# Exponentials by heads and the bound on v on ScalarE, pooled q and k by products, and a new table of priorities

## The chip, the cores and the metric

The program runs on one core of one Trainium2 chip. The metric is the device time of one execution in microseconds; the kernel before took 1002.84 us (median of three runs, 1001.24 to 1004.5). The engines are PE (TensorE matrix products, with PEld for its weight loads), DVE (VectorE), ACT (ScalarE), POOL (GpSimd) and SP (SyncE, which issues the DMAs). SBUF is the working memory; PSUM has eight banks, into which PE writes.

## The reference, cut to what matters

The input is four batches of 8 heads, 576 positions, head width 64. Attention has two branches that are added; two expert layers follow.

```
q_d, k_d, v_d = means of q, k, v over groups of 4 positions      # 144 pooled positions
out_d     = softmax(q_d k_d^T / 8) v_d,  each row repeated 4 times
out_local = softmax(q k^T / 8, only where |i - j| < 4) v
x = out_up + out_local                     # 2304 tokens x 512
x = ((x w_a) * (x w_b)) w_out              # d_ff 1536
h = x w_in ; g = max(h,0) + alpha*min(h,0) ; out = g w_out2      # d_ff 2048
```

The weights are held in 64-bit words and are brought to 32-bit and then split in pairs of f16 parts inside the kernel.

## The kernel before, in words

**Attention.** A batch is cut in six tiles of 96 query positions (TQ), each with a window of 104 key positions (WK); 24 tiles in all, the first six being batch 0. For a tile, `turn` (line 678) transposes q and k on PE, ScalarE copies them out of PSUM, and VectorE sums each group of four positions into the pooled q and k. `bound` (line 693) takes the largest magnitude of v on VectorE. `soft` (line 707) adds the band mask and the eight heads' products in two PSUM banks, takes the row maxima on VectorE, subtracts them into SBUF, lets ScalarE do one exponential over 96x832, sums it on VectorE, and scales by the reciprocal. `p_turn` and `av_t` (lines 731 and 740) transpose the probabilities and multiply by v. When all six tiles of a batch are turned, `g_top`, `g_minus`, `g_exp` and `g_out` do the pooled branch, `od_turn` transposes its result, `batch_scale` (line 786) turns the bound on v into a power of two, and `x_add` (line 756) adds both branches and splits the sum with that scale into two f16 parts in `xt`.

**Expert layers.** `s1(j, f)` (line 925) takes 288 tokens j and 128 columns f of the first layer: 24 products into two banks, then two operations of ScalarE and two of VectorE. Blocks 0 and 1 are batch 0: block 0 is its tiles 0 to 2, block 1 its tiles 3 to 5. `wab_chunk(c)` (line 993) prepares the weights for columns 2c and 2c+1: per chunk, two times three integer passes over 128x1024 on VectorE, two squares with a sum on ScalarE, and a split of each half on ScalarE and VectorE. `wo_words` and `split_rows` prepare the second weights in a like manner; `s2`, `s3`, `s4` are the other three layers.

**Order.** All instructions are first recorded. `on(t, ...)` puts steps in a calendar by a nominal time; that sets the order in which they are recorded, so the turns in which steps take PSUM banks, SBUF rings and the single bank `r` that `top_of` (line 465) uses. `Plan` (line 26) then gives each step a duration by a formula, a priority from what depends on it plus the offset of its name in the table `URGENT` (line 291), and lists each engine's instructions in order. The products of the expert layers hang in one fixed chain: the order of the calendar (s1(0,0), s1(0,1), s1(1,0), s1(1,1), s1(0,2), ...). On the chip each engine runs its list in order and waits on semaphores. `Plan.fill` (line 257) puts unneeded bf16 products on the identity (tile names `m<-idf`) into gaps of PE that the plan foresees, in its first 200 us.

**Banks.** PSUM has four banks `m` (expert layers; `h`, for the first turns, is the first two of them; the fourth holds the pooled v), three banks `a` (attention) and one bank `r`. The first batch's steps have calendar places 0.6 apart in the sequence that begins at line 1123; in it `batch_scale(0)` has place 23.4. `wab_chunk` stands at 8 + 10c (line 1175), so chunk 0 at 8, chunk 1 at 18, chunk 2 at 28.

Of the kernel before, what the change touches and what calls it, by code (L numbers as in the profile page):

```python
# [25 lines left out]
class Plan:  # L26
# [101 lines left out]
    def __call__(self, eng, method, *args, **kw):  # L128
        if "out" in kw:
            writes, ins = [kw["out"]], [a for a in args if hasattr(a, "ap")]  # L130
        else:
            writes, ins = [args[0]], [a for a in args[1:] if hasattr(a, "ap")]
        out = writes[0]
        for k, a in kw.items():
            if k == "accum_out":
                if a is not None:
                    writes.append(a)
            elif k != "out" and hasattr(a, "ap"):
                ins.append(a)
        o = self.group  # L140
        if o is None or eng != self.PE:
            o = self.new(eng)
        if eng == self.SP:
            el = kw["in_"]
            parts = [int(c) for _, c in el.ap]
            nb = SIZE[el.dtype]
            for c in parts:
                nb *= c
            run = min(min(int(x.ap[-1][1]) for x in (kw["out"], kw["in_"])) * SIZE[el.dtype], 4096)
            rate = 230e3 if run >= 1024 else 150e3  # L150
            o.dma = (nb / rate, 2.2)
            o.dur += 1.0
        else:
            d, o.lag = self.cost(eng, method, out, ins, kw)
            o.dur += d
        for a in ins:
            if not self.external(a):
                o.reads.append(self.region(a))
        for a in writes:
            if not self.external(a):  # L160
                o.writes.append(self.region(a))
        f = getattr(getattr(self.nc, eng), method)
        o.calls.append((f, args, kw))
        if o is not self.group:
            self.close(o)
# [116 lines left out]
    def issue(self):  # L282
        for o in self.order:
# [4 lines left out]
WAY = (0,0,0,0,0)  # L288


URGENT = {"": -180, "alphas": -80, "bs0": -40, "bs1": 120, "bs2": 35, "bs3": 140, "gexp0": -20, "gexp1": -130,
# [31 lines left out]
def kernel(  # L323
# [40 lines left out]
    FAC = 4  # L364
# [29 lines left out]
    banks["h"] = banks["m"][:2]  # L394
    nbank = dict.fromkeys(banks, 0)

    def bank(tag):
        nbank[tag] += 1
        return banks[tag][(nbank[tag] - 1) % len(banks[tag])]
# [210 lines left out]
    odt = carve(KD * NP).rearrange("p (a n) -> p a n", a=KD)  # L610
    vd.append(carve(H * (D + 1))[:HALF].rearrange("p (h d) -> p h d", h=H))
# [16 lines left out]
    def setup1():  # L628
        for t, n in ((idf, 128), (idb, WK)):
# [11 lines left out]
          channel_multiplier=-1)  # L641

# [35 lines left out]
    def turn(i, tag):  # L678

        b, s0, kb, off = win(i)  # L680
        rq, rk, _ = raw_of(i)
        qz, kz = qk_of(i)
        t = i % TPB
        for src, n, dst, acc, o in ((rq, TQ, qz, gq_z[b % 2], 0), (rk, WK, kz, gk_z[b % 2], off)):
            ps = bank(tag)[:, :H2 * n].rearrange("p (a n) -> p a n", a=H2)
            with pe():
                for p in range(H2):
                    T("transpose", ps[:, p], src[:, p * 128:(p + 1) * 128], idf[:n, :n])
            A("copy", dst, ps)
            V("tensor_reduce", out=acc[:, :, t * TP:(t + 1) * TP],  # L690
              in_=dst[:, :, o:o + TQ].rearrange("p a (n r) -> p a n r", r=FAC), axis=AX.X, op=ALU.add)

    def bound(i):
        V("tensor_reduce", out=vst[win(i)[0] % 2][:WK, i % TPB:i % TPB + 1], in_=raw_of(i)[2], axis=AX.XY,
          op=ALU.max, apply_absolute_value=True)
# [11 lines left out]
    def soft(i, tag="a"):  # L707
# [5 lines left out]
        with pe():  # L713
# [3 lines left out]
            for h in range(H):  # L717
                T("matmul", pss[h % 2][:, h // 2], qz[rows(h), h // 2], kz[rows(h), h // 2], start=False,
                  stop=(h >= H - 2))
        for g in range(2):  # L720
            hs = slice(H2 * g, H2 * g + H2)
            V("tensor_reduce", out=m[:, hs], in_=pss[g], axis=AX.X, op=ALU.max)
            V("tensor_tensor", out=p[:, hs], in0=pss[g], in1=m[:, hs].unsqueeze(2).to_broadcast([TQ, H2, WK]),
              op=ALU.subtract)
        A("activation", out=p, in_=p, func=ACTF.Exp, scale=scale)
        V("tensor_reduce", out=z, in_=p, axis=AX.X, op=ALU.add)
# [13 lines left out]
    def av_t(i, tag="a"):  # L740

        ps = bank(tag)[:, :KD * TQ].rearrange("p (a n) -> p a n", a=KD)
        with pe():
# [4 lines left out]
    def od_turn(b, tag="a"):  # L748
        for u in range(2):
# [6 lines left out]
    def x_add(i):  # L756

        b, t = divmod(i, TPB)
        p0 = i * TQ % XR
# [26 lines left out]
    def batch_scale(b):  # L786
# [6 lines left out]
        pow2_abs(vm, sxb[b], us, up=-1)  # L793
# [328 lines left out]

    add(setup1)
    add(lambda: load(0))
    add(setup2)
    add(lambda: load(1))
    add(setup3)
    for i in range(2, TPB):
        add(lambda i=i: load(i))
    for i in range(3):  # L1130
        add(lambda i=i: wab_load(i))
# [16 lines left out]

    tops(0)
    turns(2)  # L1150
    rest(0)
    turns(3)
    tops(1)
    turns(4)
    rest(1)
# [5 lines left out]
    tops(2)  # L1161
    for n in range(3):
        add(lambda n=n: g_exp(0, n), "gexp0")
    rest(2)
# [3 lines left out]
    for i in range(3):  # L1168
        add(lambda i=i: x_add(i), f"x{i}")
    head_end = len(seq) * 0.6  # L1170
    for n, (fn, name, bias) in enumerate(seq):
        on(n * 0.6, fn, name, bias)
# [128 lines left out]
    def group(name):  # L1301
        kind = name.rstrip("0123456789")
        n = name[len(kind):]
        if kind in ("turn", "bound", "soft", "pturn", "av", "v", "x", "load") and n:
            b = int(n) // TPB
            return f"{kind}@{b}" if kind in ("x", "load") else f"t@{b}" if b else f"t0@{n}"
# [45 lines left out]
```

## Time and profile before

| | |
|---|---|
| median of three runs | 1002.84 us (1001.24 to 1004.5) |
| the profiled execution | 1003.87 us, its span 1002.1 us |
| PE busy | 977.7 us (98%), 7488 instructions |
| DVE busy | 608.3 us (61%), 1293 instructions |
| ACT busy | 434.4 us (43%), 919 instructions |
| POOL busy | 39.5 us (4%) |
| chain that ended last | PE 84%, DVE 13%, issue 1%, ACT 1% |

The span is the time from the first to the last instruction that the profiler recorded; the execution's time has 1.8 us more around it. Busy time is the union of an engine's instructions. PE's busy time holds the unneeded products of `fill`. All steps are issued from one helper, so every instruction has line 285, and instructions are told apart by the tiles that they write and read (`zone` is a large SBUF tile that holds many things; `nm` and `nz` are the softmax's maxima and sums; `vst` the bound; `sx` a batch's scale).

### The profile page before, as it was taken

Reading aid. Unit: us, or ns where it says so; the run is one execution under the profiler, and the core shown is the slowest. Engines: PE = TensorE matmul, PEld = TensorE weight load, DVE = VectorE, ACT = ScalarE, POOL = GpSimd, SP = SyncE. Lnnn points to the kernel's source line nnn. Section 1 sums busy time; section 2 is a strip of 40 time slices with the busy share of each in tenths; the row PEclk is TensorE's granted clock in tenths of the full one; section 3 lists DMA queues with packets and bytes.
Section 4 is the critical chain, followed back from the end, with each engine's and each line's share of the span. In section 5 each row is a group of like instructions: output and inputs, shape, how many; then the busy total and the mean of one; then the engine's idle time right before and its main releaser. Section 6 shows DMA issues by size and latency. Waiting matters only on the chain.

```text
span 1002.1 us, 18185 instructions
## 1 busy us (share of the span) xinstructions
PE 977.7 (98%) x7488; PEld 672.5 (67%) x7488; DVE 608.3 (61%) x1293; ACT 434.4 (43%) x919; POOL 39.5 (4%) x81
## 2 busy tenths in 40 slices
PE   6988999999999999999999999999999999999998
PEld 4666777778877788777877777645546455464553
DVE  6899999876657566678987585612406135061340
ACT  3335566544424343335435364623516235162350
POOL 3001300012000200000000000000000000000000
PEclk9999999999999999999999999999999999999999
DMA  9596451144201512323343401010100100200000
GB/s 204 159 270 173 108 153 42 26 75 86 50 1 25 111 26 58 102 67 109 111 159 129 130 1 48 1 43 22 32 32 1 43 22 9 78 2 11 22 1 31
DMA packets 95938, 69.45 MB, mean 69 GB/s; under 512 B 71152, under 2 KB 78704, under 8 KB 95856
## 3 DMA queue, kind: packets, MB, share of 16 engines
q1 hardware_dynamic: 95856, 68.31, 25.2%
q8 instruction: 58, 0.95, 0.4%
q14 instruction: 24, 0.20, 0.1%
HBM read 58.86 MB, written 9.44 MB: 68 GB/s over the span
## 4 chain that ended last, share of the span: by engine, by line
PE 84%; DVE 13%; issue 1%; ACT 1%; DMA 0%; POOL 0%; DVEq 0%; POOLq 0%
PE m L285 75%; PE a L285 8%; DVE wab L285 4%; DVE zone L285 3%; DVE wo L285 2%; DVE nz L285 1%; DVE gt L285 1%; PE r L285 1%; DVE nm L285 1%; DVE tm L285 0%; DVE xt L285 0%; DMA zone<-in_v_dram 0%; DVE vst L285 0%; ACT wo L285 0%; ACT wab L285 0%
## 5 line engine op out<-in xcount | busy, mean ns | idle before, releaser
L285 PEld LDWEIGHTS <-wab 128*128 128x128 f16 x3168 | 306.4, 98 | 161.0 <-issue 4.2
L285 PE MATMUL m<-xt,wab 128*128 128x288 f16 x2304 | 296.2, 286 | 2.5 <-DVE xt L285 2.1
L285 PE MATMUL m<-xt,zone 128*128 128x384 f16 x1152 | 188.2, 326 | 0.0
L285 PE MATMUL m<-zone,wab 128*128 128x512 f16 x864 | 187.7, 379 | 0.0
L285 PEld LDWEIGHTS <-zone 128*128 128x128 f16 x1152 | 112.7, 98 | 74.9
L285 DVE SCALAR_TENSOR_TENSOR gt<-tm,nal,tm 128x384 f32<-128x384 f32 x96 | 59.3, 618 | 160.8 <-ACT tm L285 149.2
L285 PEld LDWEIGHTS <-wo 128*128 128x128 f16 x1152 | 111.8, 98 | 29.5 <-issue 0.8
L285 ACT ACTIVATE tm<-m 128x384 f32<-128x384 f32 (+1 forms) x224 | 95.3, 468 | 65.6 <-PE m L285 65.6
L285 PE MATMUL m<-gt,wo 128*128 128x288 f16 x864 | 110.3, 288 | 0.0
L285 DVE SCALAR_TENSOR_TENSOR wab<-gt,kap,wab 128x384 f16<-128x384 f32 x96 | 59.3, 618 | 58.2 <-ACT wab L285 58.2
L285 ACT ACTIVATE wab<-gt,kap 128x384 f16<-128x384 f32 x96 | 59.0, 615 | 58.1 <-DVE gt L285 58.1
L285 ACT ACTIVATE gt<-m,uf 128x512 f32<-128x512 f32 x18 | 12.4, 687 | 154.2 <-PE m L285 154.2
L285 ACT COPY zone<-a 104x384 f32<-104x384 f32 (+4 forms) x124 | 53.1, 471 | 53.1 <-PE a L285 52.8
L285 PE MATMUL a<-zone 64*96 64x104 f32 (+4 forms) x1104 | 72.8, 265 | 0.6 <-DVE zone L285 0.5
L285 PEld LDWEIGHTS a<-zone 64*96 64x96 f32 (+4 forms) x1104 | 58.4, 149 | 19.9 <-issue 14.6
L285 ACT ACTIVATE zone<-zone 96x832 f32<-96x832 f32 (+3 forms) x49 | 41.9, 855 | 51.8 <-DVE zone L285 49.0
L285 ACT COPY tm<-m 128x288 f32<-128x288 f32 x96 | 37.8, 394 | 43.1 <-PE m L285 40.7
L285 DVE SCALAR_TENSOR_TENSOR tm<-m,tm 128x288 f32<-128x288 f32 x96 | 43.0, 448 | 21.3 <-PE m L285 18.1
L285 ACT ACTIVATE gt<-tm 128x288 f16<-128x288 f32 x72 | 31.6, 440 | 44.4 <-DVE tm L285 44.3
L285 PE MATMUL a<-idf,zone 96*104 96x96 f32 (+4 forms) x392 | 41.6, 247 | 3.8 <-DVE sx L285 1.9
L285 POOL TENSOR_TENSOR zone<-zone 72x256 f32<-72x256 f32 x36 | 31.7, 893 | 307.9 <-DMA zone<-in_v_dram 167.2
L285 DVE SCALAR_TENSOR_TENSOR zone<-zone 128x512 int32<-128x512 int32 (+3 forms) x48 | 40.8, 861 | 0.4
(173 smaller groups left out, 810.5 us busy)
## 6 DMA issues: line engine op xcount, KB each, us to landing
zone<-in_moe_w_in_dram SPq DMA_DIRECT2D x8, 1024.0 KB
zone<-in_moe_w_out_dram SPq DMA_DIRECT2D x16, 512.0 KB
wo<-in_moe_w_a_dram SPq DMA_DIRECT2D x6, 1024.0 KB
wo<-in_moe_w_b_dram SPq DMA_DIRECT2D x6, 1024.0 KB
x_d<-x2s SPq DMA_DIRECT2D x8, 576.0 KB
out_dram<-gt SPq DMA_DIRECT2D x18, 256.0 KB
zone<-in_k_dram SPq DMA_DIRECT2D x21, 208.0 KB
zone<-in_v_dram SPq DMA_DIRECT2D x21, 208.0 KB
```

The costliest lines, as they stand in the source:

```text
L285: f(*args, **kw)
```

## The change: what it does

- `EXPH = (0, 1)`: in `soft` of batches 0 and 1 the maxima are multiplied by -scale, and ScalarE does eight exponentials of 96x104, straight from PSUM, with the row's maximum as bias and the row's sum as a second output. The subtraction and the sum over 832 are gone.
- `NORM = (0, 1)`: in `bound` of batches 0 and 1 ScalarE squares v with a sum; the scratch output goes into the tile's `xt_z`. `batch_scale` uses `pow2_ss` in place of `pow2_abs`.
- `POOLP = (0,)`: in `turn` of batch 0 PE multiplies the same stationary operand by the pooling matrix (24 columns) after each transpose, into the same bank, and ScalarE copies the result; the sum on VectorE is gone.
- Steps of tiles 0 to 2 (`soft`, `p_turn`, `av_t`) and of batch 0's pooled branch take five banks in turn: three `a` and the first two `m`.
- `setup4` fills an upsampling matrix on POOL, in memory that `od_turn` writes later. `JOIN` is empty, so nothing reads it.
- The loads of a tile are steps with names of their own: q and k (`in`), v (`inv`); likewise the first three weight loads (`wl`). `p_turn`, `av_t`, `v_tile` and `bound` get groups of their own in the table.
- The first batch's sequence is in another order, with places 0.4 apart in place of 0.6; `batch_scale(0)` now has place 16.8.
- The planner's figures for DMAs are others, and the table `URGENT` is new throughout.

```diff
-            rate = 230e3 if run >= 1024 else 150e3
+            rate = 300e3 if run >= 2048 else 220e3 if run >= 1024 else 195e3
-            o.dur += 1.0
+            o.dur += 0.8
...
-URGENT = {"": -180, "alphas": -80, "bs0": -40, ...
+EXPH, POOLP, NORM, JOIN = (0, 1), (0,), (0, 1), ()
+NUP = 1
+EARLY = [f"{k}{n}" for k in ("soft", "pturn", "av") for n in range(3)] + ["gtop0", "gminus0", "gexp0", "gout0", "odt0"]
+URGENT = {"b0@1": -145, "b0@2": 120, "b0@3": 35, ... "bs0": 85, ...
...
+    banks["x"] = banks["a"] + banks["m"][:2]
     def bank(tag):
+        if tag == "a" and P.name in EARLY:
+            tag = "x"
...
+    def setup4():
+        G("memset", up_m, 1.0)
+        G("affine_select", out=up_m, ...)
+        G("affine_select", out=up_m, ...)
...
@@ turn
+            pq = bk[:, H2 * n:H2 * (n + TP)].rearrange("p (a n) -> p a n", a=H2)
             with pe():
                 for p in range(H2):
                     T("transpose", ps[:, p], src[:, p * 128:(p + 1) * 128], idf[:n, :n])
+                    if b in POOLP:
+                        T("matmul", pq[:, p], src[:, p * 128:(p + 1) * 128], pool_m[:n, o // 4, 48:48 + TP], start=True,
+                          stop=True)
             A("copy", dst, ps)
+            if b in POOLP:
+                A("copy", acc[:, :, t * TP:(t + 1) * TP], pq)
+                continue
             V("tensor_reduce", out=acc[:, :, t * TP:(t + 1) * TP], ...
...
@@ bound
+        if b in NORM:
+            r = raw_of(i)[2].rearrange("p h d -> p (h d)")
+            A("activation", out=flat(xt_z[t])[:WK].bitcast(BF16)[:, :H * D], in_=r, func=ACTF.Square,
+              accum_out=vst[b % 2][:WK, t:t + 1])
+            return
...
@@ soft
+        each = i // TPB in EXPH
         for g in range(2):
             hs = slice(H2 * g, H2 * g + H2)
             V("tensor_reduce", out=m[:, hs], in_=pss[g], axis=AX.X, op=ALU.max)
+            if each:
+                V("tensor_scalar_mul", m[:, hs], m[:, hs], -scale)
+                for h in range(H2):
+                    x = H2 * g + h
+                    A("activation", out=p[:, x], in_=pss[g][:, h], func=ACTF.Exp, scale=scale, bias=m[:, x:x + 1],
+                      accum_out=z[:, x:x + 1])
+                continue
             V("tensor_tensor", out=p[:, hs], in0=pss[g], in1=m[:, hs]..., op=ALU.subtract)
-        A("activation", out=p, in_=p, func=ACTF.Exp, scale=scale)
-        V("tensor_reduce", out=z, in_=p, axis=AX.X, op=ALU.add)
+        if not each:
+            A("activation", out=p, in_=p, func=ACTF.Exp, scale=scale)
+            V("tensor_reduce", out=z, in_=p, axis=AX.X, op=ALU.add)
...
@@ the first batch's sequence
+    turns(2)
+    turns(3)
     tops(0)
-    turns(2)
-    rest(0)
-    turns(3)
+    turns(4)
     tops(1)
-    turns(4)
-    rest(1)
     turns(5)
...
-    tops(2)
...
-    rest(2)
+    tops(2)
...
+    for i in range(3):
+        rest(i)
...
-    head_end = len(seq) * 0.6
+    head_end = len(seq) * 0.4
```

## Rows read from the trace of the kernel before

**Rows 1.** Windows; columns: window, its length, busy time of each engine.

```profile
core 0: us, PE busy (x) PEld busy (x) DVE busy (x) ACT busy (x) POOL busy (x), PEclk, DMA share, GB/s
0.00:30.00 30.00, 21.75 (x165) 15.77 (x166) 18.77 (x40) 11.28 (x21) 7.85 (x45) 0.89 1.03 229
30.00:82.00 52.00, 44.87 (x467) 33.72 (x466) 50.40 (x110) 20.45 (x36) 3.96 (x5) 1.00 0.71 199
82.00:99.00 17.00, 14.80 (x139) 11.54 (x138) 17.00 (x30) 8.07 (x18) 1.53 (x2) 1.00 0.60 155
99.00:200.00 101.00, 98.45 (x922) 76.61 (x922) 98.47 (x235) 62.62 (x134) 8.14 (x6) 1.00 0.31 85
200.00:1002.00 802.00, 797.82 (x5800) 534.83 (x5798) 423.70 (x882) 331.96 (x713) 18.06 (x24) 1.00 0.18 51
```

**Rows 2.** Groups by form, PE, 0 to 210 us; columns as the page's.

```profile
L285 PE MATMUL m<-idf 128*128 128x256 bf16 x232 | 31.0, 276 | 0.0
L285 PE MATMUL a<-idf,zone 104*128 104x104 f32 x24 | 3.5, 267 | 0.0
```

**Rows 3.** Timeline; start, length, engine, operation, tiles, count.

```profile
30.98 0.14 DVE L285 TENSOR_REDUCE vm<-vst 128x1 f32<-128x6 f32 x1
...
51.80 0.38 PE L285 MATMUL r<-td,ones 2*128 2x2 f32 x2
...
59.01 4.20 PE L285 MATMUL m<-idf 128*128 128x256 bf16 x37
...
70.28 0.38 PE L285 MATMUL r<-td,ones 2*128 2x2 f32 x2
...
72.20 0.27 PE L285 MATMUL r<-idf,vm 128*1 128x128 f32 x1 [0.67 <-DVE us_ab L285]
...
77.68 0.62 ACT L285 ACTIVATE xt<-xt,sx 128x384 f16<-128x384 f32 x1 [0.62 <-DVE sx L285]
...
84.07 5.92 PE L285 MATMUL m<-xt,wab 128*128 128x288 f16 x47 [1.21 <-DVE xt L285]
...
99.33 5.92 PE L285 MATMUL m<-xt,wab 128*128 128x288 f16 x47 [0.85 <-DVE xt L285]
```

**Rows 4.** Groups by form, DVE, 0 to 210 us.

```profile
L285 DVE SCALAR_TENSOR_TENSOR wab<-wab,ws 128x1024 f16<-128x1024 f32 x12 | 15.3, 1273 | 0.0
L285 DVE SCALAR_TENSOR_TENSOR wab<-wo,wab 128x1024 int32<-128x1024 int32 x12 | 14.5, 1210 | 0.0
...
L285 DVE TENSOR_REDUCE nm<-a 96x4 f32<-96x416 f32 x24 | 13.0, 574 | 2.2 <-PE a L285 2.2
L285 DVE TENSOR_REDUCE zone<-zone 128x96 f32<-128x384 f32 x24 | 12.3, 537 | 6.8 <-ACT zone L285 6.8
...
L285 DVE TENSOR_TENSOR zone<-a,nm 96x416 f32<-96x416 f32 x18 | 9.6, 571 | 0.0
...
L285 DVE TENSOR_REDUCE nz<-zone 96x8 f32<-96x832 f32 x9 | 9.0, 1001 | 0.0
...
L285 DVE TENSOR_SCALAR wab<-wo 128x1024 int32<-128x1024 int32 x12 | 8.5, 711 | 0.0
L285 DVE TENSOR_REDUCE vst<-zone 104x1 f32<-104x512 f32 x10 | 6.5, 670 | 0.0
...
L285 DVE TENSOR_SCALAR nz<-nz 96x8 f32<-96x8 f32 x12 | 1.8, 154 | 0.0
```

**Rows 5.** Groups by form, ACT, 0 to 210 us.

```profile
L285 ACT ACTIVATE wo<-wo,rf 128x512 f16<-128x512 f32 x12 | 8.6, 721 | 5.3 <-DVE wo L285 5.1
L285 ACT ACTIVATE zone<-zone 96x832 f32<-96x832 f32 x9 | 8.1, 897 | 10.5 <-DVE zone L285 10.4
...
L285 ACT ACTIVATE x2s<-wo 128x512 bf16<-128x512 f32 x8 | 5.0, 628 | 3.0 <-DVE wo L285 2.6 <-ACT tm L285 0.4
L285 ACT ACTIVATE zone<-a 72x432 f32<-72x432 f32 x8 | 3.8, 519 | 2.7 <-PE a L285 2.7
...
L285 ACT ACTIVATION_READ_ACCUMULATOR wab<-wab 128x1 f32 x12 | 2.3, 188 | 0.0
...
L285 ACT ACTIVATE zone<-a 72x288 f32<-72x288 f32 x4 | 1.4, 398 | 0.0
```

More of the change, by code (lines that the diff above doesn't have):

```diff
@@ L285, in issue @@
                 f(*args, **kw)
-WAY = (0,0,0,0,0)
-URGENT = {"": -180, "alphas": -80, "bs0": -40, "bs1": 120, "bs2": 35, "bs3": 140, "gexp0": -20, "gexp1": -130,
[26 rows of a table removed]
+WAY = (0, 0, 0, 0, 0)
+EXPH, POOLP, NORM, JOIN = (0, 1), (0,), (0, 1), ()
+NUP = 1
+EARLY = [f"{k}{n}" for k in ("soft", "pturn", "av") for n in range(3)] + ["gtop0", "gminus0", "gexp0", "gout0", "odt0"]
+URGENT = {"b0@1": -145, "b0@2": 120, "b0@3": 35, "b0@4": 30, "b0@5": 100, "b@1": 90, "b@3": 30, "bs0": 85, "bs1": -70,
[30 rows of a table added]
 LAST = None
@@ L610 @@
     odt = carve(KD * NP).rearrange("p (a n) -> p a n", a=KD)
+    up_m = flat(odt)[:HALF, :HALF * FAC]
     vd.append(carve(H * (D + 1))[:HALF].rearrange("p (h d) -> p h d", h=H))
@@ L641, in setup1 @@
           channel_multiplier=-1)
+    def setup4():
+        G("memset", up_m, 1.0)
+        G("affine_select", out=up_m, in_=up_m, pattern=[[1, HALF * FAC]], compare_op=ALU.is_ge, fill=0.0, base=0,
+          channel_multiplier=-FAC)
+        G("affine_select", out=up_m, in_=up_m, pattern=[[-1, HALF * FAC]], compare_op=ALU.is_ge, fill=0.0,
+          base=FAC - 1, channel_multiplier=FAC)
     def setup2():
@@ L684, in turn @@
         for src, n, dst, acc, o in ((rq, TQ, qz, gq_z[b % 2], 0), (rk, WK, kz, gk_z[b % 2], off)):
-            ps = bank(tag)[:, :H2 * n].rearrange("p (a n) -> p a n", a=H2)
+            bk = bank(tag)
+            ps = bk[:, :H2 * n].rearrange("p (a n) -> p a n", a=H2)
+            pq = bk[:, H2 * n:H2 * (n + TP)].rearrange("p (a n) -> p a n", a=H2)
             with pe():
@@ L693, in bound @@
     def bound(i):
+        b, t = divmod(i, TPB)
+        if b in NORM:
[3 more added lines that the diff above has]
+            return
         V("tensor_reduce", out=vst[win(i)[0] % 2][:WK, i % TPB:i % TPB + 1], in_=raw_of(i)[2], axis=AX.XY,
@@ L742, in av_t @@
         ps = bank(tag)[:, :KD * TQ].rearrange("p (a n) -> p a n", a=KD)
+        b, t = divmod(i, TPB)
+        if b in JOIN:
+            u, c = divmod(t, TPB // 2)
+            with pe():
+                for h in range(H):
+                    T("matmul", ps[rows(h), h // 2], raw_of(i)[2][:, h], e_z[i % 2][:, pos(h)], start=(h < 2), stop=False)
+                for h in range(H):
+                    T("matmul", ps[rows(h), h // 2], od[:, u, h * D:(h + 1) * D], up_m[:, c * TQ:(c + 1) * TQ],
+                      start=False, stop=(h >= H - 2))
+            p0 = i * TQ % XR
+            split(ps, sxb[b], xt[:, :KD, p0:p0 + TQ], xt[:, KD:, p0:p0 + TQ])
+            return
         with pe():
@@ L748, in od_turn @@
     def od_turn(b, tag="a"):
+        if b in JOIN:
+            return
         for u in range(2):
@@ L758, in x_add @@
         b, t = divmod(i, TPB)
+        if b in JOIN:
+            return
         p0 = i * TQ % XR
@@ L792, in batch_scale @@
         us = const.tile([128, 1], F32, name=f"ux{b}")
-        pow2_abs(vm, sxb[b], us, up=-1)
+        (pow2_ss if b in NORM else pow2_abs)(vm, sxb[b], us, up=NUP if b in NORM else -1)
         u2b[b] = const.tile([128, 1], F32, name=f"u2{b}")
@@ L1121, in add, with add_in @@
         seq.append((fn, name, bias))
+    def add_in(i):
+        add(lambda: load(i, (0, 1)), f"in{i}")
+        add(lambda: load(i, (2,)), f"inv{i}")
     add(setup1)
-    add(lambda: load(0))
+    add_in(0)
     add(setup2)
-    add(lambda: load(1))
+    add_in(1)
     add(setup3)
+    add(setup4)
     for i in range(2, TPB):
-        add(lambda i=i: load(i))
+        add_in(i)
     for i in range(3):
-        add(lambda i=i: wab_load(i))
+        add(lambda i=i: wab_load(i), f"wl{i}")
     for i in range(2):
@@ L1168 @@
     for i in range(3):
+        rest(i)
+    for i in range(3):
         add(lambda i=i: x_add(i), f"x{i}")
-    head_end = len(seq) * 0.6
+    head_end = len(seq) * 0.4
     for n, (fn, name, bias) in enumerate(seq):
-        on(n * 0.6, fn, name, bias)
+        on(n * 0.4, fn, name, bias)
     T0 = 60.0
@@ L1303, in group @@
         n = name[len(kind):]
+        if kind in ("in", "inv", "wl"):
+            return name
         if kind in ("turn", "bound", "soft", "pturn", "av", "v", "x", "load") and n:
             b = int(n) // TPB
-            return f"{kind}@{b}" if kind in ("x", "load") else f"t@{b}" if b else f"t0@{n}"
+            if kind in ("x", "load"):
+                return f"{kind}@{b}"
+            k = "p" if kind in ("pturn", "av") else "b" if kind in ("v", "bound") else "t"
+            return f"{k}@{b}" if b else f"{k}0@{n}"
         if name[:3] in ("s1_", "s2_"):
```

56 rows, old and new, of the table URGENT are left out of this document.

## The prediction

> **What bounds the kernel now.** I read the windows first [rows 1]. Behind 200 us PE is busy 797.8 of 802.0 us: that stage is PE's own work, and nothing in the change touches it. The loss lies ahead of 200 us, where PE is idle for 8.2 us (0 to 30), 7.1 us (30 to 82), 2.2 us (82 to 99) and 2.6 us (99 to 200), 20.1 us in all. PE's busy time there also holds 232 unneeded products [rows 2]; 37 of them in one run took 4.20 us [rows 3], 0.1135 us each, so 26.3 us. Together 46.4 us of the first 200 are not needed by PE; its real work up to there is 200 - 46.4 = 153.6 us. This is all that the change can win, less what it adds.
>
> The engine that makes PE wait differs by stage [rows 1]. From 30 to 200 us DVE is busy for 165.9 of 170 us: it sets the pace. From 0 to 30 it is busy for 18.8, ACT for 11.3; there the steps wait for one another. The timeline shows a second cause [rows 3]: the bounds of all six v tiles are reduced at 30.98, but the transpose for batch 0's scale runs on PE at 72.20, behind weight chunk 1, whose products into the same bank r are at 70.28. Both use that one bank, and chunk 1 (place 18) stands ahead of the scale (23.4) in the calendar. So the first split of x starts at 77.68 and the first run of s1 at 84.07; the second, of block 1, at 99.33, since the chain asks for block 1 ahead of block 0's next columns. Chunk 0's products on r were at 51.80.
>
> **The change part by part.**
>
> *VectorE, removed.* A softmax tile loses two subtractions of 0.571 and a sum of 1.001 and gains two small multiplications, for which I take the 0.154 of a 96x8 operation [rows 4]: 2.143 - 0.308 = 1.835 us less; 12 tiles, 22.0 us. The bound loses 0.670, twelve times: 8.0 us. The pooled sums of batch 0 lose 0.537, twelve times: 6.4 us. In all 36.4 us of the 184.6 that DVE does up to 200 us [rows 1]; 148.2 stay. Of the 36.4, about 14.1 lie in the first 30 us (the sums 6.4, six bounds 4.0, the softmaxes of tiles 0 and 1 3.7).
>
> *ScalarE, added.* No row has an exponential of 104 columns. 432 columns from PSUM take 519 ns and 288 take 398 [rows 5]: 0.84 ns a column and 156 ns fixed, so 243 ns for 104. A per-row operand costs 721 - 628 = 93 ns, reading the sum 188 ns [rows 5]: 0.524 us each, 4.19 a tile. The whole exponential of 0.897 goes: +3.29 a tile, 12 tiles, 39.5 us. The bounds on v: a square over 512 with its sum is 0.628 + 0.188 = 0.816 [rows 5], twelve times 9.8 us. Twelve copies of 96 columns, by the same line 0.237 each, 2.8 us. In all +52 us on 102.4 up to 200 [rows 1], so 154.5. The bounds of the exponentials: 188 ns less each if reading the sum overlaps the next one (-18 us over 96), and 0.1 more each if short ones do not pipeline (+10 us).
>
> The Trainium skill, "ScalarE: Activation LUTs", section "What ACT_TABLE_LOAD costs", speaks against cutting one pass into eight: it gives about 280 ns fixed with one per-row operand plus 0.833 ns a column, with back-to-back instructions overlapping by some 93 ns. By the page a short exponential is 0.367 us, or 0.274 in a row of them; with the sum's reading from the row that is 3.7 to 4.4 us a tile against my 4.19, an estimate from the page that puts the 52 us at 46 to 55. The rows' fixed 156 + 93 lies between its two figures. Nothing below needs this.
>
> *PE, added.* 48 products on 24 columns, each with a stationary operand just used by a transpose. The nearest row is that transpose, 24 in 3.5 us, 0.146 each [rows 2]; at that price 7.0 us, at the least 0 where PE idles anyway. I take the 7.0, since I count PE's real work: 160.6 us up to the same state.
>
> *The gate on bank r.* Batch 0's scale goes from place 23.4 to 16.8, ahead of chunk 1 at 18 and still behind chunk 0 at 8. It then waits for chunk 0's products (51.80 before) instead of chunk 1's (70.28): up to 18.5 us earlier, so 77.68 becomes some 59 and s1 could start near 66 by that alone. What is late next is tiles 3 to 5 for block 1, and chunk 1 for columns 2 and 3.
>
> *Banks.* Tiles 0 to 2 with five banks can have their products issued without waiting for an earlier tile's exponentials. A bank of scores was held over a maximum and a subtraction, 0.574 + 0.571; now over a maximum, a multiplication and four exponentials, 0.574 + 0.154 + 2.10 = 2.83 [rows 4, 5]. For the first tiles the extra banks pay for that; for tiles 3 to 11, on three banks, nothing does (rival 3).
>
> *The rest.* The split of the loads leaves each DMA as it was, one per operand on SP, only in another order; the planner's new figures change orders, not work. `setup4` puts three operations on POOL, which does 7.85 us of set-up in the first 30 [rows 1]; they are covered unless they come ahead of the identity, and then cost one to two us once. The bound's scratch lies in `xt_z`, so a batch 1 bound waits for batch 0's split of the same tile; ACT's queue stands behind it, including evictions of s1. Between 0 and 2 us; I take 0, since batch 1's tiles come after those splits. Small operations of the scale are equally many. Behind 200 us the new table changes orders in a stage with 4.2 us of idle PE: it can gain at most that, and lose more; I take 0, with 5 us on the slower side in the range.
>
> *The sum.* Three engines share the work up to the state that the kernel had at 200 us: PE 160.6, ACT 154.5, DVE 148.2. In the first 30 us ACT has turns (12 copies, and 12 small ones), six bounds and two softmaxes: its former 11.3 less two exponentials (1.8), plus 2.8, 4.9 and 8.4, 25.6 us; as nothing can be copied in the first five, it is full there. So the first 30 us do not shrink; DVE idles there for some 20 us. DVE then ends near 148 + 20 + 2 = 170, ACT not before 160, PE not before 165 (its work and the first 4 to 5 us). None of three nearly full engines that hand work to each other stays full; before, the fullest lost 15.4 of 200. I take 180 in place of 200: PE then loses 19.4 us in place of 46.4, and pays 7.0 for products. The gate's 18.5 us points to the same size. So 20 us off the profiled execution's 1003.9 (span 1002.1 and 1.8 around it): 983.9; that execution lies 1 us above the median of 1002.84, so **983**.
>
> **Rivals.**
> 1. *More: the order was the cost.* The gate and DVE's relief add up; PE starts s1 near 60 and is full from there. State at 168, about 8 us of loss left: 32 us off, **971**. For it: PE loses only 2.6 us in 99 to 200 once it has work [rows 1]. Against: ACT at 154.5 of 168.
> 2. *ScalarE takes DVE's place in the head.* The first 30 us run long, since a chain of one softmax now has 4.19 on ACT in place of 2 x 0.571 + 0.897 + 1.001 on DVE and ACT, and turns stand in the same queue. If batch 0 is late by ACT's overhang there (25.6 in 25, then three more softmaxes, 9.9 us more), 12 to 15 of the 20 go: **996**.
> 3. *Slower: bursts on ScalarE hold up s1.* A batch 1 softmax puts eight exponentials, 4.19 us, in ACT's queue ahead of s1's evictions, and its two score banks stay closed. An s1 step takes 24 products, 5.92/48 x 24 = 2.96 us [rows 3], and two pairs of m banks give about that much grace. If the whole burst stalls PE, six tiles and the three late ones of batch 0 give 9 x 4.19 = 37.7 against the 27 regained, with 7 paid for: 17.7 worse, **1021**; at two thirds of a burst it is 25 + 7 against 27, **1008**. It decides from 20/9 = 2.2 us of stall per burst. Against it: ACT is only 62% busy in 99 to 200 [rows 1], and two halves of four exponentials leave room between them.
> 4. *Nothing moves:* the chip leaves the plan's order so that block 1 starts near 99 again, and DVE's saving becomes idle time: **1002**.
>
> **How the numbers follow.** Forecast (12 to 28 us off) 0.50; rival 1, 0.13; rival 2, 0.20; rival 3, 0.10; rival 4, 0.07. A measurement can tell about 0.3%, 3 us, from no change. Faster is the forecast with rivals 1 and 2, 0.83; the same 0.07; slower 0.10. The range from 967 to 1001 leaves out rival 3, half of rival 4, and a few in a hundred below.
>
> **What would show it.** Right: the scale's transpose on r well before 72, close behind chunk 0's; the first s1 run near 60 to 68 and block 1's near 75 to 80 in place of 99; unneeded products and idle PE up to 200 near 20 us together; DVE some 36 us less and ACT some 52 more over the span; short exponentials near 0.33 with 0.19 for the sum. Wrong: ACT full from 5 us on and PE waiting for its copies until past 80 (rival 2); PE waits in 80 to 180 ended by ACT's evictions or score banks (rival 3); an idle PE behind 200 us beyond 4 us (the table).

## The result and the profile after

The changed kernel takes **1014.89 us** (median of 6 runs, 1009.26 to 1020.04) against 1003.22 for the kernel before, measured beside it (6 runs, 1001.24 to 1007.26). The ratio is **1.0112, 95% interval 1.0068 to 1.0157**: about 1% slower, where 983 was forecast. The profiled execution took 1013.9 us, span 1012.2. Of e2's ten runs below three were slow (1018.32 to 1020.47) and are left out.

The page of the changed kernel first: busy time, share and count of each engine, and the granted clock in 40 slices.

```profile
PE 990.8 (98%) x7481; PEld 687.7 (68%) x7481; DVE 580.3 (57%) x1257; ACT 464.1 (46%) x1135; POOL 50.4 (5%) x84
...
PEclk9969999999999999999999999999999999999999
```

PE was busy for 977.7 us before, DVE for 608.3, ACT for 434.4. VectorE was relieved (28.0 less) and ScalarE loaded (29.7 more); but PE is 13.1 us busier, although it runs fewer of the unneeded products. These are in the groups by form (PE, 0 to 210 us), beside the transposes that the prediction took its price from:

```profile
L285 PE MATMUL m<-idf 128*128 128x256 bf16 x129 | 17.0, 281 | 0.0
...
L285 PE MATMUL a<-idf,zone 104*128 104x104 f32 x24 | 3.5, 267 | 0.0
```

129 in place of 232 [rows 2]: by the groups' busy time 31.0 - 17.0 = 14.0 us less (by the 0.1135 a product of the prediction 11.7). So the needed work of PE grew by 13.1 + 14.0 = 27.1 us (24.8 at that price), where 7.0 was forecast. Its idle time over the span went from 24.4 to 21.4. Busy and idle time together are the span, so 13.1 more and 3.0 less give the 10.1 us by which the spans differ (1012.2 - 1002.1).

The windows of the changed kernel, at the places of [rows 1]:

```profile
0.00:30.00 30.00, 25.91 (x154) 24.49 (x156) 1.44 (x8) 10.77 (x39) 8.85 (x48) 1.00 1.01 230
30.00:82.00 52.00, 47.09 (x369) 35.27 (x367) 37.31 (x89) 24.65 (x87) 5.10 (x3) 0.80 0.53 144
82.00:99.00 17.00, 13.64 (x149) 10.86 (x149) 16.93 (x32) 11.42 (x37) 3.75 (x4) 1.00 0.53 171
99.00:200.00 101.00, 96.16 (x916) 75.61 (x914) 96.11 (x230) 81.71 (x255) 13.18 (x6) 1.00 0.41 110
200.00:1012.00 812.00, 807.96 (x5909) 541.51 (x5905) 428.48 (x900) 335.50 (x720) 19.48 (x24) 1.00 0.18 51
```

In the first 30 us DVE does 1.44 us of work, in place of 18.77: it waits for PE. ACT, which the prediction held to be full there, does 10.77. PE is the busy one, 25.91, and with fewer instructions than before (154 for 165). The same view at places that follow the stages:

```profile
4.00:37.00 33.00, 32.91 (x174) 28.24 (x175) 3.77 (x11) 12.84 (x56) 5.48 (x29) 1.00 0.86 196
37.00:47.50 10.50, 8.65 (x65) 5.10 (x64) 8.59 (x23) 3.68 (x12) 0.00 (x0) 1.00 0.01 2
47.50:68.00 20.50, 19.86 (x147) 16.89 (x148) 12.36 (x29) 8.11 (x27) 0.00 (x0) 0.50 0.60 175
68.00:111.00 43.00, 34.75 (x384) 28.16 (x382) 42.81 (x85) 29.03 (x91) 15.73 (x8) 1.00 0.77 221
```

PE is full from 4 to 37 us. The granted clock reads 1.00 there, but that cell can't be read so: the trace's first record of the clock is at 37.3 us, and ahead of it the view fills in 1.00. What the clock was, the products tell. The timeline of PE (start, length, tiles, count), a transpose and its pooled product in turn; a pooled product shows as two instructions:

```profile
4.09 0.39 PE L285 MATMUL m<-idf,gt 96*128 96x96 f32 x1 [4.09 <-POOL one L285]
4.28 0.51 PE L285 MATMUL m<-pool_m,gt 96*128 96x24 f32 x2
4.62 0.40 PE L285 MATMUL m<-idf,gt 96*128 96x96 f32 x1
4.81 0.51 PE L285 MATMUL m<-pool_m,gt 96*128 96x24 f32 x2
5.15 0.40 PE L285 MATMUL m<-idf,gt 96*128 96x96 f32 x1
...
37.77 0.28 PE L285 MATMUL m<-idf,zone 96*128 96x96 f32 x1
37.89 0.33 PE L285 MATMUL m<-pool_m,zone 96*128 96x24 f32 x2
38.06 0.28 PE L285 MATMUL m<-idf,zone 96*128 96x96 f32 x1
...
70.70 0.38 PE L285 MATMUL r<-td,ones 2*128 2x2 f32 x2
...
74.35 0.27 PE L285 MATMUL r<-idf,vm 128*1 128x128 f32 x1
...
86.59 6.05 PE L285 MATMUL m<-xt,wab 128*128 128x288 f16 x48
...
111.49 0.28 PE L285 MATMUL m<-xt,wab 128*128 128x288 f16 x1
112.64 7.39 PE L285 MATMUL m<-xt,wab 128*128 128x288 f16 x59 [0.86 <-DVE xt L285]
```

From one transpose to the next it is 0.53 us (5.15 - 4.62) in all pairs up to 32.7, and 0.29 in the four behind 37.3 (38.06 - 37.77): half speed, 1.2 GHz, and then 2.4 GHz. From 47.5 to 68 the clock is at 0.50 again, by its own records, after a stretch in which PE was idle for 1.85 of 10.5 us. Then the late marks: batch 0's scale at 74.35 (72.20 before, and some 54 forecast), s1 of block 0 from 86.59 (its first product stood at 82.58 before, the run of [rows 3] at 84.07), of block 1 from 111.49 (98.19 before, the run of [rows 3] at 99.33).

The scale now stands right behind chunk 0's products on bank r, as planned; but these came at 70.70 in place of 51.80 [rows 3]. The preparation of chunk 0's weights uses no result of the turns, but its first pass stands on DVE behind operations that wait for PE, and DVE runs its list in order. Before, and then in the changed kernel:

```profile
35.13 0.68 DVE L285 TENSOR_SCALAR wab<-wo 128x1024 int32<-128x1024 int32 x1
...
44.73 0.68 DVE L285 TENSOR_SCALAR wab<-wo 128x1024 int32<-128x1024 int32 x1
```

The Trainium skill, "TensorE: Matmul & The Clock Gate", section "HAM oscillation — how this bites in real kernels", puts a fallen clock down to stretches in which PE stands idle. The fall at 47.5 is in line with that, though no single wait ahead of it was longer than 1.01 us. The low clock from 4 to 37, with 0.09 us idle, is not a fall behind idle time, and that section does not account for it.

ScalarE, POOL and VectorE in the timeline of the changed kernel:

```profile
76.46 0.34 ACT L285 ACTIVATE zone<-a,nm 96x104 f32<-96x104 f32 x1 [0.57 <-DVE nm L285]
76.71 0.19 ACT L285 ACTIVATION_READ_ACCUMULATOR zone<-a,nm 96x1 f32 x1
76.80 0.33 ACT L285 ACTIVATE zone<-a,nm 96x104 f32<-96x104 f32 x1
...
76.82 5.32 POOL L285 TENSOR_TENSOR zone<-zone 72x256 f32<-72x256 f32 x3 [67.35 <-DMA zone<-in_v_dram]
...
77.03 0.19 ACT L285 ACTIVATION_READ_ACCUMULATOR zone<-a,nm 96x1 f32 x1
77.12 0.33 ACT L285 ACTIVATE zone<-a,nm 96x104 f32<-96x104 f32 x1
...
80.68 0.69 DVE L285 TENSOR_SCALAR nz<-nz 96x8 f32<-96x8 f32 x1
```

VectorE's small multiplications in its groups by form, 0 to 210 us:

```profile
L285 DVE TENSOR_SCALAR nm<-nm 96x4 f32<-96x4 f32 x24 | 3.6, 156 | 0.0
L285 DVE TENSOR_SCALAR nz<-nz 96x8 f32<-96x8 f32 x12 | 3.5, 291 | 1.0 <-ACT zone L285 1.0
```

In the timeline one exponential starts 0.32 to 0.34 us behind the last (77.12 - 76.80), the reading of the sum included: 0.524 was forecast. The new multiplications take 0.156, near the 0.154 of the price. The old small one on nz takes 0.291 in the mean in place of 0.154 [rows 4].

### The profile page after: what moved, and what is told of

It is laid out like the page before. It is cut to its first block, busy times and chain, and to the rows that moved or that the text cites. A ratio compares the mean times of both kernels' runs of the same rounds, so it can differ in the third digit from the quotient of the medians.

```text
span 1012.2 us, 18352 instructions
## 1 busy us (share of the span) xinstructions
PE 990.8 (98%) x7481; PEld 687.7 (68%) x7481; DVE 580.3 (57%) x1257; ACT 464.1 (46%) x1135; POOL 50.4 (5%) x84
## 4 chain that ended last, share of the span: by engine, by line
PE 89%; DVE 9%; issue 1%; ACT 1%; POOL 0%; DVEq 0%; POOLq 0%
PE m L285 79%; PE a L285 10%; DVE wab L285 3%; DVE zone L285 2%; DVE xt L285 1%; PE r L285 1%; DVE wo L285 1%; DVE nm L285 1%; ACT zone L285 0%; DVE tm L285 0%; DVE nz L285 0%; DVE gt L285 0%; DVE vst L285 0%; DVE us_ab L285 0%; POOL pool_m L285 0%
## 5 line engine op out<-in xcount | busy, mean ns | idle before, releaser
L285 ACT ACTIVATE gt<-m,uf 128x512 f32<-128x512 f32 x18 | 12.4, 687 | 151.4 <-PE m L285 151.4
L285 PEld LDWEIGHTS a<-zone 64*96 64x96 f32 (+4 forms) x1046 | 60.1, 155 | 17.7 <-issue 13.7
L285 ACT COPY zone<-a 104x384 f32<-104x384 f32 (+4 forms) x119 | 50.7, 473 | 32.0 <-PE a L285 31.8
L285 ACT ACTIVATE zone<-zone 128x512 bf16<-128x512 f32 (+4 forms) x48 | 38.9, 812 | 43.3 <-DVE zone L285 39.6
L285 POOL TENSOR_TENSOR zone<-zone 72x256 f32<-72x256 f32 x36 | 41.5, 1165 | 309.8 <-DMA zone<-in_v_dram 231.3
L285 ACT ACTIVATE gt<-tm 128x288 f16<-128x288 f32 x72 | 31.9, 443 | 51.1 <-DVE tm L285 50.7
L285 PEld LDWEIGHTS a<-idf,zone 96*104 96x104 f32 (+4 forms) x384 | 33.9, 132 | 13.3 <-DVE zone L285 3.9
```

Source lines behind the costliest of these rows:

```text
L285: f(*args, **kw)
```

## The experiments

Three explanations stood at the start: the pooled products on PE, at the clock that they run at; the exponentials on ScalarE; and the order of the work (sequence, banks, table). Each run was timed beside the kernel before; ratios are to it. That kernel's median lay between 1001.65 and 1003.22 from one round to the next, so differences between runs of different rounds are good to 1 or 2 us.

| run | median us | ratio (95%) |
|---|---|---|
| e1: after without pooled products | 997.52 | 0.9954 (0.9939 to 0.9969) |
| e2: 46 unneeded products among the turns | 1013.99 | 1.0080 (1.0044 to 1.0117) |
| e3: after without short exponentials | 1023.16 | 1.0212 (1.0196 to 1.0228) |
| e4: before with pooled products alone | 1016.94 | 1.0146 (1.0096 to 1.0196) |
| e5: 110 unneeded products among the turns | 1009.62 | 1.0067 (1.0041 to 1.0094) |
| e6: e1 with the old bound | 996.37 | 0.9945 (0.9923 to 0.9966) |
| e7: only order, banks and table | 1023.52 | 1.0199 (1.0157 to 1.0242) |
| e8: e1 with tiles 3 to 5 on five banks | 988.64 | 0.9857 (0.9823 to 0.9891) |
| e9: before with the scale ahead of chunk 1 | 1006.80 | 1.0054 (1.0034 to 1.0074) |
| e10: before with short exponentials alone | 999.41 | 0.9967 (0.9955 to 0.9980) |
| e11: e8 with the old bound | 992.90 | 0.9912 (0.9886 to 0.9937) |
| e12: e8 with pooled products | 1023.00 | 1.0194 (1.0133 to 1.0256) |
| e13: after, filled to hold the clock | 1004.33 | 1.0014 (1.0002 to 1.0026) |
| e14: e12, filled to hold the clock | 1008.63 | 1.0058 (1.0045 to 1.0071) |
| e15: e8 with a few unneeded products | 989.68 | 0.9872 (0.9859 to 0.9886) |

**e1**, the pooled sums back on VectorE, all else as after:

```diff
-EXPH, POOLP, NORM, JOIN = (0, 1), (0,), (0, 1), ()
+EXPH, POOLP, NORM, JOIN = (0, 1), (), (0, 1), ()
```

> The changed kernel with batch 0's pooled q and k summed on VectorE again (POOLP empty), all else as changed. Theory A (the pooled products and their transposes run at the low clock and make PE the bound up to 45 us): the head gets shorter by some 10 us or more, PE is not full between 5 and 36 us, block 1's first s1 run starts near 100 in place of 111.5, the time falls from 1014 to about 1000 to 1005. Theory B (the exponentials by heads make the head late, whatever PE does): the time stays at 1010 to 1018.

17.4 us faster than the changed kernel, and faster than before. The window of e1 that answers to 4 to 37 us above:

```profile
4.00:37.00 33.00, 30.56 (x264) 21.65 (x265) 25.64 (x60) 21.32 (x79) 5.46 (x29) 1.00 1.00 242
```

The first products of s1 in the timeline of e1:

```profile
65.69 6.05 PE L285 MATMUL m<-xt,wab 128*128 128x288 f16 x48
...
96.77 0.29 PE L285 MATMUL m<-xt,wab 128*128 128x288 f16 x1
```

In the same 33 us PE runs 264 instructions in place of 174, and DVE has 25.64 us of work in place of 3.77. Its turns end at 19.7 us in place of 38.5. Block 0 starts at 65.69, just where the prediction had put it; block 1 starts at 96.77, where 75 to 80 was forecast. So the products cost the time; that it is their clock, e2, e5 and e13 had to tell.

**e2** and **e5**, unneeded products ahead of the first turn and behind each half turn of batch 0; e2 has 10 and 3:

```diff
+    warm = lambda n: (nc.tensor.matmul, (banks["m"][2][:, :256], ib[:, :128], ib), dict(start=True, stop=True))
...
+            w.calls, w.name = [warm(0)] * 10, "fill"
...
+            w.calls, w.name = [warm(0)] * 3, "fill"
```

> The changed kernel in the same order, with ten unneeded bf16 products on PE ahead of its first transpose and three after each turn's half of batch 0 (46 in all). Theory A with the clock as cause: the granted clock rises to 2.4 GHz well before 37 us, a transpose with its pooled product takes near 0.29 in place of 0.53 us, and batch 0's turns end near 24 in place of 38 us; the time falls by 8 to 14 us, to 1000 to 1006. Rival (the pair is slow by itself, two kinds of product in turn): pairs stay at 0.53 us and the time rises by the added products, up to 5 us.

Inconclusive: the first record of the full clock came at 41.1 us, and the pairs ahead of it still stood 0.53 apart, so the edit didn't do what it was to do. e5 has more of them: the kernel that ran has 50 ahead and 5 behind each half turn, 110 in all, not the 30 and 90 of the expectation.

> As e2_warm (the changed kernel, same order), with 30 unneeded bf16 products ahead of the first transpose and five after each half of a turn of batch 0, 90 in all. Theory A with the clock as the cause: the clock rises to 2.4 GHz before 15 us, pairs of transpose and pooled product fall from 0.53 to near 0.29 us, and in spite of the added products the turns end near 30 us in place of 37; the time is 1000 to 1008. If more dummies still do not lift the clock: pairs stay at 0.53, the turns end near 50 us and the time is 1022 to 1030.

Now the clock was full from 7.0 to 44.6 and the pairs some 0.28 apart; the turns ended near 34.5 instead of 38.5, and the time fell by 5.3 us in spite of 110 more products (the intervals of the ratios overlap). From 44.6 to 65 the clock was at half, as in the changed kernel.

**e3**, the old softmax in the changed kernel (`EXPH = ()`), and **e10**, the new one alone in the kernel before:

> The changed kernel with one exponential of 96x832 per tile again (EXPH empty), all else as changed. Theory A: the head keeps its slow turns, so block 1 starts no earlier than 111 and the time is 1012 to 1025, DVE being fuller by 22 us. Theory B: the time falls towards 1003.

> The kernel before with the exponentials by heads for batches 0 and 1, and nothing else. If the 22.0 us of VectorE that they take away are the gain, in any order: 6 to 15 us faster, 988 to 997. If they pay only with the new order and table (e7_none to e6_nonorm showed 27 us there): within 4 us of 1002. If bursts on ScalarE hold up s1's evictions: slower, 1006 or more.

With the short exponentials taken away the changed kernel is 8 us slower; put alone into the kernel before they gain 3.3 us. They are a gain, and not the cause.

**e4**, the kernel before with the pooled products alone:

```diff
+                    if b == 0:
+                        T("matmul", pq[:, p], src[:, p * 128:(p + 1) * 128], pool_m[:n, o // 4, 48:48 + TP], start=True,
+                          stop=True)
...
+                A("copy", acc[:, :, t * TP:(t + 1) * TP], pq)
+                continue
```

> The kernel before with batch 0's pooled q and k by products, as in the change, and nothing else. Theory A: the turns slow down and the clock falls in the first 40 us; 8 to 15 us slower, 1011 to 1018. If the pooled products are harmless by themselves (the old order has unneeded products among the turns that keep the clock up): within 4 us of 1003, since DVE loses 6.4 us of work.

14 us slower, under the old order, the old table and the old softmax. Its pairs too stand 0.53 apart, and its first record of the full clock comes at 48.3 us. This edit alone is enough to turn the sign.

**e6** (e1 with `NORM = ()`) and **e7** (`EXPH`, `POOLP` and `NORM` all empty) peel off the rest:

> As e1_nopool with the bound on v on VectorE again (NORM empty). If the bound on ScalarE is worth its 8.0 us of DVE: 2 to 6 us slower than e1_nopool's 997.5, 1000 to 1003. If ScalarE's ten extra us in the head cost as much as they free: within 2 us of e1_nopool.

> As e1_nopool with EXPH, NORM and POOLP all empty: what is left of the change is the order, the five banks, the split loads and the new table. If the gain of e1_nopool comes from the exponentials and the bound on ScalarE (30 us less on DVE): 1006 to 1015. If it comes from the order and the gate on bank r: 997 to 1002.

The bound on ScalarE is worth nothing in e1 (1.2 us, intervals overlap). Order, banks and table by themselves lose 20 us, and under that order the exponentials are worth 27 (e7 against e6).

**e9**, the old kernel with the scale ahead of chunk 1, by the chunk's place alone:

```diff
-        on(8.0 + 10.0 * c, lambda c=c: wab_chunk(c), f"wab{c}", 0.0)
+        on(24.0 if c == 1 else 8.0 + 10.0 * c, lambda c=c: wab_chunk(c), f"wab{c}", 0.0)
```

> The kernel before, with weight chunk 1's calendar place moved from 18 to 24, behind batch 0's scale at 23.4; nothing else. The scale's transpose on bank r then stands ahead of chunk 1's. If the gate on r was worth what the prediction gave it: the transpose near 54 in place of 72, the first s1 run near 66 to 70 in place of 84, the time 6 to 15 us less, 988 to 997. If block 1 (99.3 us, tiles 3 to 5) sets the pace and not the scale: the first s1 run comes earlier, block 1 stays within 4 us of 99 and the time within 4 us of 1002.

The timeline of PE in e9:

```profile
54.13 0.27 PE L285 MATMUL r<-idf,vm 128*1 128x128 f32 x1
...
70.15 6.05 PE L285 MATMUL m<-xt,wab 128*128 128x288 f16 x48
...
100.03 6.26 PE L285 MATMUL m<-xt,wab 128*128 128x288 f16 x48
```

The gate opened 18.1 us earlier (54.13 for 72.20), as the prediction reckoned (18.5); block 0's first product came 12.4 us earlier (70.15 for 82.58); block 1's came 1.8 us later, and the kernel was 0.5% slower. The whole gain at the gate was lost behind it: the chain needs block 1. That block 1 waits for tiles 3 to 5, e8 tests, in the new order.

**e8** goes at these tiles: e1, with tiles 3 to 5 on five banks as well and their softmaxes placed right behind the head.

```diff
-EXPH, POOLP, NORM, JOIN = (0, 1), (0,), (0, 1), ()
-EARLY = [f"{k}{n}" for k in ("soft", "pturn", "av") for n in range(3)] + ["gtop0", "gminus0", "gexp0", "gout0", "odt0"]
+EXPH, POOLP, NORM, JOIN = (0, 1), (), (0, 1), ()
+EARLY = [f"{k}{n}" for k in ("soft", "pturn", "av") for n in range(6)] + ["gtop0", "gminus0", "gexp0", "gout0", "odt0"]
...
-        on(t, lambda i=i: soft(i), f"soft{i}", 2.0)
+        on(head_end + 0.2 * n, lambda i=i: soft(i), f"soft{i}", 2.0)
```

> As e1_nopool, with tiles 3 to 5 recorded together (their scores one after the other, then the rest) and on five banks as tiles 0 to 2 are. If the turns of the three banks are what strings these tiles behind one another (scores of tiles 3, 4, 5 at 48, 64 and 78 us in e1_nopool) and so holds block 1 to 97.9: block 1 starts at 80 to 88, and the time falls by 4 to 10 us, to 988 to 993. If VectorE's load sets block 1's start: it stays near 97 and the time within 3 us of 997.5.

The score maxima of tiles 3 to 5 (two a tile) in the timeline of DVE in e1:

```profile
48.12 1.07 DVE L285 TENSOR_REDUCE nm<-a 96x4 f32<-96x416 f32 x2
64.70 1.08 DVE L285 TENSOR_REDUCE nm<-a 96x4 f32<-96x416 f32 x2 [1.40 <-PE a L285]
78.61 1.08 DVE L285 TENSOR_REDUCE nm<-a 96x4 f32<-96x416 f32 x2 [0.56 <-PE a L285]
```

The same in e8, and PE's first products of block 1 there:

```profile
47.68 0.57 DVE L285 TENSOR_REDUCE nm<-m 96x4 f32<-96x416 f32 x1
48.18 0.57 DVE L285 TENSOR_REDUCE nm<-a 96x4 f32<-96x416 f32 x1
48.74 1.07 DVE L285 TENSOR_REDUCE nm<-a 96x4 f32<-96x416 f32 x2
...
54.97 0.58 DVE L285 TENSOR_REDUCE nm<-m 96x4 f32<-96x416 f32 x1
55.58 0.53 DVE L285 TENSOR_REDUCE nm<-m 96x4 f32<-96x416 f32 x1
...
82.42 1.64 PE L285 MATMUL m<-xt,wab 128*128 128x288 f16 x12
```

In e1 tiles 3 to 5 come one by one, 14 to 17 us apart; in e8 all three come within 8.5 us (47.68 to 56.1); block 1 starts at 82.42 in place of 96.77, and the kernel takes **988.64 us**, 8.9 us less than e1 and 1.4% less than the kernel before. This version beats both kernels.

**e11** (e8 with `NORM = ()`), **e12** (e8 with `POOLP = (0,)`):

> As e8_tiles (988.6) with the bound on v on VectorE (NORM empty). e6 against e1 showed no difference: 986 to 992. If ScalarE has become the bound of the head with the tiles close together, taking 9.8 us from it gains: 980 to 986.

> As e8_tiles with batch 0's pooled q and k by products (POOLP (0,)): the whole change plus tiles 3 to 5 together on five banks. Theory A: the products cost their 14 to 17 us here too, 1000 to 1008, with the clock low until 35 to 50 us. If they only hurt while the tiles are strung out: within 4 us of 988.6.

With the tiles early the bound on ScalarE is worth some 4 us (the intervals just overlap), so ScalarE isn't the limit even with all of it. The pooled products cost 34 us here, twice the 17.4 that they cost against e1; e14 tells a part of why.

**e13**, the whole change in its own order, with unneeded products put where PE thins out (24 ahead, 2 behind each half turn, 4 to 8 behind the steps of the pooled branch and behind `soft2`):

```diff
+    after = {'turn0': 2, 'turn1': 2, 'turn2': 2, 'turn3': 2, 'turn4': 2, 'turn5': 2, 'gtop0': 6, 'gminus0': 8, 'gexp0': 6, 'soft2': 4, 'gout0': 4}
+    order, n = [], 24
```

> The changed kernel in its own order, all parts on, with unneeded bf16 products spread so that PE's clock should stay up: 24 ahead of the first transpose, 2 behind each half of a turn of batch 0, and 4 to 8 behind each step of its pooled branch and tile 2's scores. If the low clock is the whole cost of the pooled products (14 to 17 us): no 1.2 GHz stretch between 10 and 70 us, pairs at 0.29 us, block 1's first s1 run near 98 to 100 in place of 111.5, the time 998 to 1004. If the products' own work on PE, ahead of everything in the turns, costs as much again: block 1 near 104 to 106, the time 1005 to 1010.

The windows of e13 from 37 to 68 us:

```profile
37.00:47.50 10.50, 9.49 (x83) 6.73 (x82) 7.23 (x10) 4.07 (x9) 0.00 (x0) 0.84 0.59 201
47.50:68.00 20.50, 19.37 (x245) 17.07 (x244) 17.75 (x45) 11.90 (x47) 0.09 (x1) 1.00 0.78 167
```

PE's timeline in e13:

```profile
9.36 0.28 PE L285 MATMUL m<-idf,gt 96*128 96x96 f32 x1
9.47 0.33 PE L285 MATMUL m<-pool_m,gt 96*128 96x24 f32 x2
9.64 0.28 PE L285 MATMUL m<-idf,gt 96*128 96x96 f32 x1
...
102.58 7.51 PE L285 MATMUL m<-xt,wab 128*128 128x288 f16 x60
```

The pairs are 0.28 us apart at 9 us (9.64 - 9.36), the turns end at 27.6, the clock is full from 47.5 to 68 (0.84 in the 10.5 us ahead of that), block 1 starts 8.9 us earlier, and the time falls by **10.6 us** though PE runs more products (241 unneeded ones in place of 129). The runs also lie closer together (1002.47 to 1005.54). So the clock is worth 10.6 us in this kernel; e5, which mended only the first stretch, got back half of that. Most of it must belong to the pooled products, but not surely all: e1, without them, is not at full clock throughout either (0.83 granted from 47.5 to 68), and filling might have helped it as well. The 6.8 left against e1 is about the size of the products' own work at full clock: 48 pairs take 48 x 0.285 = 13.7 us, 48 transposes alone 7.0 at the 0.146 of [rows 2], or 4.9 by their spacing in the kernel before (four in 0.41, from 9.64 to 10.05). The filling is among the 6.8 too, and the runs don't part the two.

**e14** (e12 with the same filling) and **e15** (e8 with 10 ahead and a few in the pooled branch):

> As e12_tpool (whole change, tiles 3 to 5 together; 1023.0) with the same added products as e13_clock. By the clock alone: within 6 us of e8_tiles' 988.6, so 988 to 995. If the pooled products cost by their work too: 996 to 1006.

> As e8_tiles (988.6) with ten unneeded products ahead of the first transpose, 6 behind the step of the maxima and 4 behind each of the pooled exponentials. e8_tiles has 1.2 GHz up to 11.2 and from 52.1 to 55.5 and 59.0 to 62.4 us. If those stretches still cost: 984 to 987. If PE has slack there: within 2 us of 988.6.

In e14 the filling gives back 14.4 of e12's 34 us. The other 20 remain open: the clock is still at half from 39 to 49 us, the order of steps is another one too (block 1 at 96.85 against 82.42 in e8), and I didn't separate that from the products' own work. In e15 nothing is gained: in e8, without the products, its short stretches of half clock are no cost worth mending.

## Why the prediction was wrong

- **Two steps failed, *PE, added* and *The sum*.** The forecast was 27 us regained by PE less 7.0 for the products. Without the products the change gained 5.6 us (e1 against the kernel beside it), and the products cost 17.4. The 21.4 that the sum had too much and the 10.4 that the products had too little are the 32 us between 983 and 1014.89. It was the products that turned the sign.
- ***PE, added*.** It priced 48 products at 0.146 each, a row read at full clock: 7.0 us, which was also the upper end. At full clock that is near (0.285 a pair less 0.10 to 0.146 for its transpose). But 44 of the 48 pairs ran at 1.2 GHz: 44 x 0.533 + 4 x 0.285 = 24.6 us, where the 48 transposes alone take 7.5 in the kernel before (busy time of their groups), so 17.1 more. Some 10 of the 27.1 are left (8 of the 24.8); other products in the slow stretches can be seen to pay (those on `gt` and `pool_m` take 1072 ns in the mean, 592 before), but I haven't counted them one by one. No term and no rival asked at which clock the stretch would run; the slower outcome came from PE and from none of the rivals.
- ***The sum*.** It took 19.4 us of idle and unneeded time on PE up to 200 us in place of 46.4. Counted in the same way the changed kernel has 31.9 (17.2 idle, 129 x 0.1135 unneeded), e1 has 37.1 and e8 30.3. DVE did get the relief that was forecast, but in e1 block 1 started only 1.4 us earlier by it (96.77 for 98.19), so PE went on waiting.
- **"The first 30 us do not shrink", since ACT is full there: wrong engine.** PE was full, ACT at 10.77 of 30, and the last turn ended at 38.5 us where it had ended near 23. All of batch 0 stands behind these turns, and PE's added work there is on the path nearly one for one: the turns end 18.8 us earlier in e1 and 10.9 in e13, and the times are 17.4 and 10.6 less.
- ***The gate on bank r*: the mechanism right, its worth wrong.** e9 moved the scale by 18.1 us and gained nothing. "What is late next is tiles 3 to 5 for block 1" stood in the step, without a price; it should have been the term. In 12 of the 17 kernels the profiled execution ends 901 to 907 us behind block 1's first product: before 98.19 and 1003.87, e1 96.77 and 997.87, e8 82.42 and 988.33, after 111.49 and 1013.9. In e3, e7, e11, e12 and e14 it ends 913 to 928 us behind it: there PE is idle for 4.8 to 15.8 us between that product and 200 us, in the twelve for 1.2 to 4.5. So an early block 1 does not suffice (e11 has the earliest, at 77.64, and takes 992.9).
- ***Banks*:** five banks for tiles 0 to 2 alone left tiles 3 to 5 strung out; giving them all five, with an earlier place, was worth 8.9 us (e8).
- ***VectorE, removed*: right in size.** Over the span the removed groups come to 38.9 us (subtractions 12.8, sums of exponentials 12.0, bounds 7.9, pooled sums 6.2) and the multiplications to 3.6: 35.3, against 36.4. DVE's busy time fell by only 28.0. Some operations there got longer (those on nz 1.8 us in all, the scaling of the probabilities 1.5); where the rest went the groups don't show. The exponentials by heads do gain (e3, e7, e10).
- ***ScalarE, added*: too dear.** 29.7 us in place of 52. The 96 exponentials take 31.6 us by their groups, 0.33 each, against the 50.3 taken; the reading of the sum overlaps the next exponential, which was the lower bound given. So rivals 2 and 3, which lived on ScalarE's load, had little ground. The Trainium skill, "ScalarE: Activation LUTs", section "What ACT_TABLE_LOAD costs", gives by its figures an estimate of 0.274 for one in a row of them; the measured 0.33 from one to the next, which holds the sum too, is nearer to that than to my 0.524.
- ***The rest*:** the order, banks and table were put at nothing. Without the three moves they lose 20 us (e7); with the exponentials they gain (e6 against e10, 996.37 and 999.41), so their worth can't be stated apart from the three moves. Behind 200 us PE is idle for 4.0 us, as before (4.2): there the new table cost nothing.

## What to carry to other kernels

Work moved to PE has two prices, one at each clock level: read the spacing of like instructions in the stretch it goes to, and bound the sum with both. The kernel before showed both for the transposes: four of 104 columns took 0.71 us from 4.27 on, 0.41 from 9.64 on. Before a gate is priced, look for what its successor waits for next; the gain is the distance to that, which here was nothing. If such products are wanted, unneeded ones between them can pay (10.6 us here), but the cheaper answer was to leave the pooled sums on VectorE, which stood idle. And an engine that runs a list in order passes a delay on to work that needs nothing from the late step, as chunk 0's weights showed.

## What the runs showed of the hardware

- PE busy for 32.91 of 33 us, with transposes and 24-column products in fp32, stayed at 1.2 GHz until 37.3 us; with 46 unneeded bf16 products among them (e2) until 41.1; with 24 ahead and 2 behind each half turn (e13) the clock was full from 6.0 to 40.1 us.
- A window's granted clock of 1.00 ahead of the first clock record says nothing: in the changed kernel it stands over products at half speed.
- Some small operations on VectorE take longer while POOL adds: 0.69 us in place of 0.15 for 96x8 at 80.68, under POOL's additions from 76.82. Others in that stretch do not (0.13 for 128x1 at 81.29). The mean addition on POOL rose as well, 0.893 to 1.165.
